# Attention and token-MLP on one core: scores one matmul ahead over five banks, and ScalarE's and the loads' order changed around the MLP

## The chip, the core and the metric

The kernel runs on one core of a Trainium2 chip. TensorE (PE) multiplies matrices into the eight banks of PSUM, ScalarE (ACT) computes functions and copies, VectorE (DVE) reduces and combines, GpSimd (POOL) works on on-chip memory alone, and SyncE (SP) issues transfers; ACT and POOL issue transfers too. Each engine runs its own queue of instructions in order and waits on semaphores for the others. The metric is the time of one execution on the device in microseconds (us); less is better.

## What is computed

```python
x = A_x                                       # 1 x 2048 x 640
g = sigmoid((x * gate_w).sum(-1, keepdims=True))
# a: attention with 32 heads of 20 channels
q, k, v = split(x @ wqkv)                     # 32 heads each
p = softmax(einsum("bhqd,bhkd->bhqk", q, k) * 20 ** -0.5)
a = concat_heads(p @ v) @ wo
# b: an MLP over the tokens, shared by the channels
h = layernorm(x)
u = gelu(einsum("bsd,sf->bdf", h, w1) + b1)   # F = 1728
b = (einsum("bdf,fs->bds", u, w2) + b2) transposed to tokens x channels
out = g * a + (1 - g) * b
```

Inputs and output are float32. Products that need more than one pass of the fast format are made of a high and a low part: `a = ah + al`, and `ah*bh + ah*bl + al*bh`.

## The kernel before, in words

The program has four stages that follow one another on TensorE.

**Projections (0 to 226 us).** Ten blocks of 128 rows of Q and K transposed, four tiles of 512 tokens each (`qk_unit`, L286: 15 matmuls), and V in two halves. The first two blocks of Q and of K come first, then V, then the rest. Each tile of Q and K is split into a high part (ACT, tile `evh`) and a low part (DVE, `evl`) and stored to DRAM by SP; for the first three K blocks (384 rows, `c` = 0 to 2) SP also stores them to `kd_d`, and for every second tile the difference to the tile before it (`kf`, `dh`). There are two buffers of `evh` and `evl` each and one of `kf`, so the next use of a buffer waits for its stores. V needs its own weights split (`split_wv`, L357) by ACT and DVE, in the same queues. Mean and variance of the layer norm, and the gate `g_t`, are made beside V (L378 to 414).

**MLP (226 to 774 us)**, in two halves `d` of 320 channels (`mlp`, L577). In each half `u` has 14 tiles of 128 hidden units and `y` 16 tiles of 128 tokens. Each step is one `pair64`: two matmuls of 64 rows that run side by side. The weights come in 120 chunks a half: `w_raw` (L450) loads chunk k into a `wr` tile, `w_split` (L462) makes its high part on ACT (`wh`) and its low part on POOL (`wl`), `w_need` keeps loads nine and splits four chunks ahead. Chunks 0 to 3 (`AHEAD = 4`) are fetched by ACT's queue during the projections into tiles that exist by then; from chunk 4 on, `wr`, `wh` and `wl` lie in the pool `gp`, which takes over the memory of the projections' pool `p1` (L510 to 513). `u_evac` (L526) copies a finished pair of sums on ACT, and puts off the rest through the list `soon`: POOL's addition after 6 steps, the Gelu (`u_gelu`, L545) after 18. `settle` (L518) counts `soon` down once a step. At the end of each `y` tile, `y_evac` does the same; in the first half the input of the second is loaded, normalised on DVE and split beside it (`h_load`, `h_norm`, `h_split`), with the last two splits behind the loop (L621 to 624).

Beside the MLP runs the first part of a second stream, the row maxima of the attention scores: `s_next` (L166) issues one matmul `s` of 512 columns (L193) and what reads it. They come two at a time, 1082 over the 2592 steps. For half of the heads three in eight go through ACT (`s_over`: a Relu into the tile `ov`, L206) and then DVE (`s_two`); the others are reduced by DVE alone (L199). Four PSUM banks rotate for `s`. A Relu stands in ACT's queue where its matmul was issued.

**Attention loop (774 to 1779 us).** 16 pairs of heads, 32 iterations `it` each. An iteration takes 128 keys and 1024 queries: four score matmuls `st` (L789; heads j = 0, 1, whose rows 0 and 64 let a neighbour run beside them), an exponential of each on ACT into a tile `p` (L792), two matmuls of the maxima of a later pair in between as long as there are any (`s_next`; the turn of j keeps neighbours on different rows), and then `pv_flush` (L720): the products with V of the iteration before, four tiles `p` by two passes each. Banks: `st` rotates over four (`tag="st", bufs=4`), but the third score of each iteration has a bank of its own (`s3`); two are for `s` and one for `pv`.

**Output projection (1779 to 1863 us)**, with the gate and the MLP's result added by DVE.

What sets the order: PE's instructions stand as written throughout, ACT's and DVE's from L325, POOL's and SP's from L417 on. So a wait at the head of one queue holds all that is written behind it.

## Time and profile before

| | us |
|---|---|
| three runs | 1860.23, 1867.78, 1869.33 (median 1867.78) |
| the profiled execution | 1864.34 |
| its span, first to last instruction | 1862.6 |
| busy in it: PE | 1832.7 (98%) |
| ACT | 1510.6 (81%) |
| DVE | 1241.1 (67%) |
| POOL | 632.2 (34%) |
| PE's weight loads, beside its matmuls | 1121.4 (60%) |

How to read the rows: L12 is line 12 of the kernel. A group's row has engine, operation, output<-inputs, shapes and count; a timeline's row has start and duration in us, then the same, and in brackets how long the engine was idle before and what ended that; a row of waits has who waited for whom, the total in us, how often, and the longest. PEld are PE's weight loads, SPq and ACTq what those queues issue. Matmuls overlap, so PE counts as busy where it is not at its full rate.

### The profile page before, as it was taken

The page shows a single profiled execution, that of the slowest core. Times are in us where ns is not written, and L with a number is a line of the kernel's source. Part 1 is how long each engine was busy: PE and PEld are TensorE (multiplying, and loading weights), DVE is VectorE, ACT ScalarE, POOL GpSimd, SP SyncE. Part 2 cuts the span into 40 slices and gives each one's busy share as a digit, 9 for nine tenths or more (in the row PEclk, how much of TensorE's full clock was granted, in tenths as well). Part 3 has the DMA queues.
Part 4 walks back from the last instruction along what each step waited for, and adds up shares of the span by engine and source line. Part 5 has one row for each costly group of instructions (what it writes and reads, how often), then busy time and mean ns, then how long its engine had stood idle before and what let it go on. Part 6 is the DMA issues. An engine that isn't in the chain of part 4 may idle for free. (4 is left out here: it accounts for less than half of the span.)

```text
span 1862.6 us, 40444 instructions
## 1 busy us (share of the span) xinstructions
PE 1832.7 (98%) x14978; PEld 1121.4 (60%) x14978; DVE 1241.1 (67%) x2407; ACT 1510.6 (81%) x3046; POOL 632.2 (34%) x882
## 2 busy tenths in 40 slices
PE   9999999999999999999999999999999999999998
PEld 7898789999899999633333333333333333333278
DVE  5303278898888888866666666666766666667137
ACT  4244378887788777599999999999999999999920
POOL 1012367778777767302111211121322121212210
PEclk9999999999999999999999999999999999999999
DMA  9657866466665555225222232142263322201363
GB/s 310 196 163 235 257 155 174 134 166 194 183 168 148 148 148 168 72 58 137 58 46 61 60 80 57 27 109 59 52 126 67 71 62 57 71 14 23 129 215 132
DMA packets 156695, 223.00 MB, mean 120 GB/s; under 512 B 65998, under 2 KB 92382, under 8 KB 153070
## 3 DMA queue, kind: packets, MB, share of 16 engines
q1 hardware_dynamic: 133888, 186.94, 36.8%
q0 software_dynamic: 13824, 18.81, 4.5%
q10 hardware_dynamic: 8784, 14.65, 2.4%
q8 instruction: 118, 1.93, 0.4%
q14 instruction: 81, 0.66, 0.1%
HBM read 165.43 MB, written 54.54 MB: 118 GB/s over the span
## 5 line engine op out<-in xcount | busy, mean ns | idle before, releaser
L199 DVE TENSOR_REDUCE mx<-s 128x1 f32<-128x512 f32 x1280 | 832.8, 686 | 303.8 <-PE st L789 165.1
L792 ACT ACTIVATE p<-st 128x512 f32<-128x512 f32 x2048 | 1004.0, 822 | 0.0
L726 PE MATMUL pv<-p,v 128*32 128x512 f32 x4096 | 567.6, 605 | 0.1
L789 PEld LDWEIGHTS st<-qs_True,ks_True 62*128 62x128 f32 x2048 | 245.9, 184 | 530.2 <-issue 426.8
L789 PE MATMUL st<-qs_True,ks_True 62*128 62x512 f32 x2048 | 508.9, 436 | 0.1
L193 PE MATMUL s<-ks_False,qs_False 60*128 60x512 f32 x1152 | 326.1, 407 | 15.0 <-ACT ov L206 10.6
L193 PE MATMUL s<-sk,sq 60*128 60x512 f32 x896 | 325.0, 442 | 0.0
L43 POOL TENSOR_TENSOR wl<-wr,wh 128x512 fp32r<-128x512 f32 x228 | 276.6, 1217 | 119.0 <-ACT wh L40 75.5
L213 DVE CUSTOM_DVE_ANT_0 ov<-s,ov 128x512 f32<-128x512 f32 x384 | 263.5, 687 | 60.2 <-PE s L193 54.0
L206 ACT ACTIVATE ov<-s 128x512 f32<-128x512 f32 x384 | 224.9, 597 | 84.0 <-PE s L193 79.6
L713 POOL DMA_DIRECT2D o_d<-oev x128 | 66.8, 522 | 619.7 <-DVE oev L707 603.8
L48 PE MATMUL y<-gh,wh 64*128 64x320 f32 x896 | 203.5, 307 | 0.0
L48 PE MATMUL y<-gl,wh 64*128 64x320 f32 x832 | 195.2, 307 | 0.0
L48 PE MATMUL y<-gh,wl 64*128 64x320 f32 x832 | 194.2, 306 | 0.0
L193 PEld LDWEIGHTS s<-ks_False,qs_False 60*128 60x128 f32 x1152 | 171.2, 185 | 30.4 <-ACT ov L206 17.5
L40 ACT ACTIVATE wh<-wr 128x512 fp32r<-128x512 f32 (+2 forms) x246 | 147.2, 601 | 46.4 <-DMA wr<-in_wqk_dram 31.0
L726 PEld LDWEIGHTS pv<-p,v 128*32 128x32 f32 x4096 | 102.2, 108 | 125.9 <-issue 116.7
L48 PE MATMUL u<-hl,wh 64*128 64x320 f32 x864 | 166.3, 307 | 0.0
L48 PE MATMUL u<-hh,wh 64*128 64x320 f32 x864 | 166.3, 307 | 0.0
L48 PE MATMUL u<-hh,wl 64*128 64x320 f32 x800 | 155.4, 307 | 0.0
L48 PEld LDWEIGHTS y<-gh,wh 64*128 64x128 f32 x896 | 143.6, 185 | 0.9
L48 PEld LDWEIGHTS y<-gl,wh 64*128 64x128 f32 x832 | 134.8, 185 | 0.7
(124 smaller groups left out, 2123.0 us busy)
## 6 DMA issues: line engine op xcount, KB each, us to landing
wr<-in_w_dram SPq DMA_DIRECT2D x196, 256.0 KB
ks_True<-k_d SPq DMA_DIRECT2D x96, 160.0 KB
qs_True<-q_d SPq DMA_DIRECT2D x192, 80.0 KB
qs_False<-q_d SPq DMA_DIRECT2D x108, 80.0 KB
sk<-k_d SPq DMA_DIRECT2D x42, 160.0 KB
sq<-q_d SPq DMA_DIRECT2D x84, 80.0 KB
v_d<-vt SPq DMA_DIRECT2D x32, 168.0 KB
v<-v_d SPq DMA_DIRECT2D x16, 336.0 KB
```

Of the source, the lines that this page charges most:

```text
L40: nc.scalar.activation(hi, src, AF.Copy)
L43: (lo_eng or nc.vector).tensor_sub(lo, src, hi.bitcast(F32))
L48: nc.tensor.matmul(ps[k], a[r], b[r], start=start, stop=stop)
L193: nc.tensor.matmul(ps, qs[half][r, t * P:(t + 1) * P], ks[r, kc * 512:(kc + 1) * 512], start=True, stop=True)
L199: nc.vector.tensor_reduce(mx[:, slot, j, t: t + 1], ps, axis=AX.X, op=OP.max)
L206: nc.scalar.activation(over[j, kc], ps, AF.Relu)
L213: nc.vector.tensor_tensor_reduce(ov, ps, ov, 1.0, -3.0e38, OP.add, OP.max, mx[:, slot, j, t: t + 1])
L713: nc.gpsimd.dma_start(o_d[DH * h: DH * h + DH, cols], ev[r: r + DH, :])
L726: nc.tensor.matmul(pv[r: r + 32, :], v_tiles[p][:, kt, 10 * j: 10 * j + 32], pts[j, c], start=(kt == 0), stop=(kt == NT - 1))
L789: nc.tensor.matmul(ps, ks[r, kt * P:(kt + 1) * P], qs[qh][r, c * 512:(c + 1) * 512], start=True, stop=True)
L792: nc.scalar.activation(pt, ps, AF.Exp, scale=SCALE)
```

## The change

Seven edits. (1) A score matmul `st` and its exponential are issued one place earlier: the first of iteration n stands before the `pv` of iteration n-2 instead of after it. The order of the heads within an iteration becomes 1, 0, 1, 0, and the scores rotate over five banks one after the other (`st0` to `st3` and `s3`); the tag `st` is cut into four tags of one bank, whose order of use elsewhere is as before. (2) A Relu of the maxima is issued two steps after its matmul. (3) Gelu comes 30 steps behind its tile instead of 18, but for the last of a half. (4) The second half's inputs are loaded three tiles ahead, normalised one ahead and split in the step of their own tile. (5) Weight chunks 4 to 7 are fetched by ACT's queue, into six tiles (`q4`) that held weights of the projections, and chunk 3 is split before the last Q/K tile. (6) The Gelu table is loaded right after the gate, by a Gelu of a tile that nobody reads any more (`ssq`), and the Exp table at the second half's fifteenth output tile instead of its fourth. (7) For the first two K blocks the four stores of the differences go through POOL's queue.

```diff
     def st_tile(shape, name):
-        return psum.tile(shape, F32, tag="st", bufs=4, name=name)
+        n = st_count[0] % 4
+        st_count[0] += 1
+        return psum.tile(shape, F32, tag=f"st{n}", bufs=1, name=name)
...
     def s_over(p, half, t, j, kc, over):
         def f():
             ps = s_mm(p, half, t, j, kc)
-            over[j, kc] = s_pool[0].tile([P, 512], F32, tag="over", bufs=3, name=f"ov{p}_{half}_{t}_{j}_{kc}")
-            nc.scalar.activation(over[j, kc], ps, AF.Relu)
+
+            def relu():
+                over[j, kc] = s_pool[0].tile([P, 512], F32, tag="over", bufs=3, name=f"ov{p}_{half}_{t}_{j}_{kc}")
+                nc.scalar.activation(over[j, kc], ps, AF.Relu)
+
+            soon.append([2, relu])
         return f
...
-        nc.sync.dma_start(kd_d[0, rows, cols], hi.bitcast(F32))
-        nc.sync.dma_start(kd_d[1, rows, cols], lo.bitcast(F32))
+        put = nc.gpsimd.dma_start if c < 2 else nc.sync.dma_start
+        put(kd_d[0, rows, cols], hi.bitcast(F32))
+        put(kd_d[1, rows, cols], lo.bitcast(F32))
...
-        nc.sync.dma_start(kd_d[0, rows, cols], dh.bitcast(F32))
-        nc.sync.dma_start(kd_d[1, rows, cols], kd)
+        put(kd_d[0, rows, cols], dh.bitcast(F32))
+        put(kd_d[1, rows, cols], kd)
...
     nc.vector.tensor_mul(b2o, b2_t, omg)
+    nc.scalar.activation(ssq, ssq, AF.Gelu_apprx_tanh)
...
         if k < AHEAD:
             raw = p1.tile([P, 4, P], F32, tag="xr", bufs=2, name=f"wr{k}")
+        elif k < 2 * AHEAD:
+            raw = q4([P, 4, P], F32, f"wr{k}")
         else:
             raw = gp.tile([P, 4, P], F32, tag="wr", bufs=8, name=f"wr{k}")
-        (nc.scalar if k < AHEAD else nc.sync).dma_start(raw[:, :n, :m], src)
+        (nc.scalar if k < 2 * AHEAD else nc.sync).dma_start(raw[:, :n, :m], src)
...
+        if n == 23:
+            w_split(3)
         qk_unit(m, w[m], q)
...
-        if n in (22, 23):
-            w_split(n - 20)
+        if n == 22:
+            w_split(2)
+            w_raw(4)
+            w_raw(5)
...
-            soon.append([18, lambda: u_gelu(f, xg, gh, gl)])
+            soon.append([18 if f == f_order[-1] else 30, lambda: u_gelu(f, xg, gh, gl)])
...
             for f in f_order:
+                if d == 0 and f == f_order[-1]:
+                    for i in range(3):
+                        h_load(1, i)
...
-                if d and t == 3:
+                if d and t == NT - 2:
                     nc.scalar.activation(eps_t, eps_t, AF.Exp)
                 if d == 0:
-                    if t > 1:
-                        hs[t - 2] = h_split(1, t - 2)
-                    if t > 0:
-                        h_norm(1, t - 1)
-                    h_load(1, t)
-            if d == 0:
-                hs[NT - 2] = h_split(1, NT - 2)
-                h_norm(1, NT - 1)
-                hs[NT - 1] = h_split(1, NT - 1)
+                    if t == 0:
+                        h_norm(1, 0)
+                    if t + 1 < NT:
+                        h_norm(1, t + 1)
+                    hs[t] = h_split(1, t)
+                    if t + 3 < NT:
+                        h_load(1, t + 3)
...
+    def st_op(i):
+        g, n = divmod(i, 4)
+        p, it = divmod(g, 32)
+        qh, kt = divmod(it, NT)
+        ks, qs = st_src[p]
+        j, c = 1 - n % 2, n // 2
+        r = slice(64 * j, 64 * j + 3 * DH + 2)
+        ps = psum.tile([P, 512], F32, tag="s3" if i % 5 == 4 else f"st{i % 5}", bufs=1, name=f"st{p}_{it}_{j}{c}")
+        nc.tensor.matmul(ps, ks[r, kt * P:(kt + 1) * P], qs[qh][r, c * 512:(c + 1) * 512], start=True, stop=True)
+        pt = lp.tile([P, 512], F32, tag="pt", bufs=12, name=f"p{p}_{it}_{j}{c}")
+        nc.scalar.activation(pt, ps, AF.Exp, scale=SCALE)
+        pts.setdefault(g, {})[j, c] = pt
+
+    st_op(0)
...
             for n in range(4):
-                st_op((n + turn) % 2, n // 2, s3_tile if n == 2 else st_tile)
+                i = 4 * (p * 32 + it) + n + 1
+                if i < NP * 128:
+                    st_op(i)
                 if n < take:
                     s_next()
...
-            pend.append((p, qh, kt, pv, pts))
+            pend.append((p, qh, kt, pv, pts.pop(p * 32 + it)))
```

Three places show how instructions move. First ACT where the projections end and the MLP begins; `evh9_3` is the high part of the last Q/K tile, `ov` a Relu, `wr4` to `wr7` are weight chunks 4 to 7 and `wh4` the split of chunk 4. Before:

```order
L40 ACTIVATE wtmp1_1440<-wr2_2097 128x512 [waits DMAHW5_49]
L40 ACTIVATE evh9_3_2163<-qk9_3_2147 128x512 [waits DMAHW3_49,DVE_49,PE_49]
L40 ACTIVATE wtmp1_1440<-wr3_2121 128x512 [waits DMAHW2_49]
L206 ACTIVATE ov0_0_0_1_0_2192<-s0_0_0_1_0_2190 128x512 [waits PE_49]
L206 ACTIVATE ov0_0_0_1_2_2204<-s0_0_0_1_2_2202 128x512 [waits PE_49]
L206 ACTIVATE ov0_0_0_0_0_2224<-s0_0_0_0_0_2222 128x512 [waits PE_49]
L40 ACTIVATE wh4_2232<-wr4_2177 128x512 [waits DMAHW4_49,DMAHW5_49,DMAHW1_49,DMAHW6_49,DMAHW0_49,DMAHW7_49,DVE_49,Pool_49]
L206 ACTIVATE ov0_0_1_1_0_2260<-s0_0_1_1_0_2258 128x512 [waits PE_49]
```

And with the change:

```order
L40 ACTIVATE wtmp1_1441<-wr2_2098 128x512 [waits DMAHW5_49]
L471 DMA wr4_2148<-in_w1_dram 128x512
L471 DMA wr5_2150<-in_w1_dram 128x512
L40 ACTIVATE wtmp1_1441<-wr3_2122 128x512 [waits DMAHW2_49]
L40 ACTIVATE evh9_3_2170<-qk9_3_2154 128x512 [waits DMAHW3_49,DVE_49,PE_49]
L471 DMA wr6_2182<-in_w1_dram 128x512 [waits DMAHW1_49]
L471 DMA wr7_2184<-in_w1_dram 128x512
L212 ACTIVATE ov0_0_0_1_0_2197<-s0_0_0_1_0_2191 128x512 [waits PE_49]
L212 ACTIVATE ov0_0_0_1_2_2212<-s0_0_0_1_2_2203 128x512 [waits PE_49]
L212 ACTIVATE ov0_0_0_0_0_2229<-s0_0_0_0_0_2223 128x512 [waits PE_49]
L40 ACTIVATE wh4_2233<-wr4_2148 128x512 [waits DMAHW5_49,DMAHW4_49,DMAHW6_49,DMAHW2_49,DMAHW7_49,DVE_49,Pool_49]
L212 ACTIVATE ov0_0_1_1_0_2268<-s0_0_1_1_0_2259 128x512 [waits PE_49]
```

Four loads came into ACT's queue, two of them between the last Q/K tile and the first Relu; the split of chunk 4 keeps its place and a list of waits, since its output lies in memory that the projections use.

Second, ACT in the first half's `u`, at the Gelu of tile 4 (`xg0_4`). Before:

```order
L40 ACTIVATE wh28_3409<-wr28_3151 128x512
L206 ACTIVATE ov0_1_7_1_0_3423<-s0_1_7_1_0_3421 128x512
L546 ACTIVATE xg0_4_3345<-xg0_4_3345,b1_t_83 128x320
L40 ACTIVATE gh0_4_3343<-xg0_4_3345 128x320
L206 ACTIVATE ov0_1_7_1_2_3443<-s0_1_7_1_2_3441 128x512
L40 ACTIVATE wh29_3456<-wr29_3202 128x512
```

And with the change:

```order
L40 ACTIVATE wh28_3410<-wr28_3152 128x512
L212 ACTIVATE ov0_1_7_1_0_3431<-s0_1_7_1_0_3422 128x512
L212 ACTIVATE ov0_1_7_1_2_3448<-s0_1_7_1_2_3439 128x512
L40 ACTIVATE wh29_3454<-wr29_3201 128x512
L212 ACTIVATE ov0_1_7_0_0_3471<-s0_1_7_0_0_3465 128x512
L562 ACTIVATE xg0_4_3346<-xg0_4_3346,b1_t_83 128x320
```

The Gelu and the copy `gh` went behind two more Relus and a split.

Third, PE in one iteration of the loop; the digits of a score are pair, iteration, head and half of the queries. Before:

```order
L193 MATMUL s12_1_3_1_3_21393<-sk12_18505,sq12_1_18507 128x512 [waits DVE_49]
L789 MATMUL st8_19_10_21396<-qs8_True_1_20084,ks8_True_20082 128x512 [waits Activation_49]
L193 MATMUL s12_1_3_0_3_21400<-sk12_18505,sq12_1_18507 128x512 [waits DVE_49]
L789 MATMUL st8_19_01_21403<-qs8_True_1_20084,ks8_True_20082 128x512 [waits Activation_49]
L789 MATMUL st8_19_11_21407<-qs8_True_1_20084,ks8_True_20082 128x512
L726 MATMUL pv8_1_21299<-p8_18_00_21364,v8_20268 32x512
L726 MATMUL pv8_1_21299<-p8_18_01_21378,v8_20268 32x512
L726 MATMUL pv8_1_21299<-p8_18_10_21371,v8_20268 32x512
L726 MATMUL pv8_1_21299<-p8_18_11_21382,v8_20268 32x512 [waits Activation_49]
L789 MATMUL st8_20_00_21415<-qs8_True_1_20084,ks8_True_20082 128x512
```

And with the change:

```order
L787 MATMUL st8_19_00_21394<-qs8_True_1_20089,ks8_True_20087 128x512 [waits Activation_49]
L197 MATMUL s12_1_3_1_3_21398<-sk12_18510,sq12_1_18512 128x512 [waits DVE_49]
L787 MATMUL st8_19_11_21401<-qs8_True_1_20089,ks8_True_20087 128x512 [waits Activation_49]
L197 MATMUL s12_1_3_0_3_21405<-sk12_18510,sq12_1_18512 128x512 [waits DVE_49]
L787 MATMUL st8_19_01_21408<-qs8_True_1_20089,ks8_True_20087 128x512 [waits Activation_49]
L787 MATMUL st8_20_10_21412<-qs8_True_1_20089,ks8_True_20087 128x512 [waits Activation_49]
L743 MATMUL pv8_1_21304<-p8_18_00_21369,v8_20273 32x512
L743 MATMUL pv8_1_21304<-p8_18_01_21383,v8_20273 32x512
L743 MATMUL pv8_1_21304<-p8_18_10_21361,v8_20273 32x512
L743 MATMUL pv8_1_21304<-p8_18_11_21376,v8_20273 32x512
```

The first score of iteration 20 moved ahead of the `pv` of iteration 18; each score now waits for the exponential that read its bank, and `pv` waits for none of its own.

More of the change, by code (lines that the diff above doesn't have):

```diff
@@ L71, in st_tile @@
     def st_tile(shape, name):
-        return psum.tile(shape, F32, tag="st", bufs=4, name=name)
+        n = st_count[0] % 4
+        st_count[0] += 1
+        return psum.tile(shape, F32, tag=f"st{n}", bufs=1, name=name)
+    st_count = [0]
     def s_tile(shape, name):
@@ L721, in pv_flush @@
         while pend:
-            p, qh, kt, pv, pts = pend.pop(0)
+            p, qh, kt, pv, pt = pend.pop(0)
             for j in range(2):
@@ L725, in pv_flush @@
                     r = 32 * (2 * j + c)
-                    nc.tensor.matmul(pv[r: r + 32, :], v_tiles[p][:, kt, 10 * j: 10 * j + 32], pts[j, c],
+                    nc.tensor.matmul(pv[r: r + 32, :], v_tiles[p][:, kt, 10 * j: 10 * j + 32], pt[j, c],
                                      start=(kt == 0), stop=(kt == NT - 1))
@@ L757, in o_late @@
         return o_part(q, slice((NC - 1) * P, D), 1, 512, "l", 4, nc.scalar, nc.vector)[0]
-    turn = given = 0
+    given = 0
+    pts = {}
+    def st_op(i):
[11 more added lines that the diff above has]
+    st_op(0)
     LEFT = NP * 128 + 2 - S_AHEAD
     for p in range(NP):
-        ks, qs = st_src[p]
+        qs = st_src[p][1]
         if 8 <= p < 8 + NC:
@@ L783, in gated_mix @@
                 pv = psum.tile([P, 512], F32, tag="pv", bufs=1, name=f"pv{p}_{qh}")
-            pts = {}
-            def st_op(j, c, tile):
-                r = slice(64 * j, 64 * j + 3 * DH + 2)
-                ps = tile([P, 512], f"st{p}_{it}_{j}{c}")
-                nc.tensor.matmul(ps, ks[r, kt * P:(kt + 1) * P], qs[qh][r, c * 512:(c + 1) * 512],
-                                 start=True, stop=True)
-                pt = lp.tile([P, 512], F32, tag="pt", bufs=12, name=f"p{p}_{it}_{j}{c}")
-                nc.scalar.activation(pt, ps, AF.Exp, scale=SCALE)
-                pts[j, c] = pt
             take = min(LEFT - given, 2)
             for n in range(4):
-                st_op((n + turn) % 2, n // 2, s3_tile if n == 2 else st_tile)
+                i = 4 * (p * 32 + it) + n + 1
+                if i < NP * 128:
+                    st_op(i)
                 if n < take:
@@ L802, in gated_mix @@
                 s_finish()
-            turn = (turn + take) % 2
             pv_flush()
```

## The prediction

> **What bounds the kernel now.** I read the windows of 100 us first, then the groups and one iteration of the attention loop on the timeline, then the waits of TensorE window by window. Columns of a window: its length, busy us (instructions) of PE, weight loads, DVE, ACT and POOL, granted clock, DMA share, GB/s.
>
> ```profile
> core 0: 1862.6 us, clock 0.995
> 300.00:400.00 100.00, 99.49 (x1215) 97.25 (x1214) 87.66 (x223) 81.23 (x162) 75.85 (x80) 1.00 0.57 156
> 900.00:1000.00 100.00, 100.00 (x719) 34.99 (x717) 68.74 (x113) 100.00 (x205) 18.37 (x40) 1.00 0.33 75
> L792 ACT ACTIVATE p<-st x2048: 592/827/858, 774.4 to 1777.5; 128x512 f32<-128x512 f32 x187
> ```
>
> There are two regimes. Up to 774 us TensorE has matmuls without pause and the others serve it; from 774.4 to 1777.5 us ScalarE computes 2048 exponentials, and is busy 100 of 100 us. The first stage can gain where TensorE waits; the loop only if an exponential's turn gets shorter.
>
> Whether it can is read from runs of exponentials that nothing separates: the first with score and maximum matmuls beside it, the second after those have run out. A run of n lasts n-1 turns and one full length (0.83).
>
> ```profile
> 1299.62 7.20 ACT L792 ACTIVATE p<-st 128x512 f32<-128x512 f32 x14
> 1737.39 23.36 ACT L792 ACTIVATE p<-st 128x512 f32<-128x512 f32 x47
> 575.08 1.07 ACT L206 ACTIVATE ov<-s 128x512 f32<-128x512 f32 x2
> ```
>
> (7.20-0.83)/13 = 0.490 us, and (23.36-0.83)/46 = 0.490 us, though TensorE's work differs. Two Relus of this size in the MLP, back to back: 1.07 less one of 0.59 is 0.48. So 0.49 is ScalarE's own pace; 2048 x 0.490 = 1003.5 us is the whole loop (1777.5-774.4 = 1003.1 from first start to last).
>
> The Trainium skill ("ScalarE: Activation LUTs", What happens when an `exp` ACTIVATE runs) states one element per cycle and lane once the pipe is full, 0.833 ns. By that the estimate is 512 x 0.833 = 427 ns a turn; the trace shows 490, and nothing of this size under 0.48.
>
> **The loop.** An iteration in TensorE's rows:
>
> ```profile
> 1301.48 0.19 PEld L789 LDWEIGHTS st<-qs_True,ks_True 62*128 62x128 f32 x2 [0.19 <-ACT p L792]
> 1301.91 0.20 PEld L726 LDWEIGHTS pv<-p,v 128*32 128x32 f32 x8 [0.24 <-issue]
> 1302.95 0.18 PEld L789 LDWEIGHTS st<-qs_True,ks_True 62*128 62x128 f32 x1 [0.84 <-issue]
> 1303.29 0.40 PE L789 MATMUL st<-qs_True,ks_True 62*128 62x512 f32 x1
> 1303.44 0.19 PEld L789 LDWEIGHTS st<-qs_True,ks_True 62*128 62x128 f32 x2 [0.19 <-ACT p L792]
> 1303.52 0.42 PE L789 MATMUL st<-qs_True,ks_True 62*128 62x512 f32 x2
> ```
>
> From one 1301.48 to the next 1303.44 is 1.96 us = 4 x 0.49: last pair of scores to pv 0.43, pv 1.04, first pair 0.34, second to third pair 0.15. TensorE waits 0.19 of it for an exponential, so its own chain lies between 1.77 and 1.96. With the change the four scores, two maxima and pv remain, shifted by one score; the fifth-last exponential now frees the last score's bank, and the same exponential frees pv. A score has one turn (0.49) more in hand, and ScalarE loses the extra semaphore instructions that stand before half of its exponentials, but the turn was 0.490 with them. I take 0.4 us of gain, for starts that come late once in a while; bounds: 0, and 2048 x (0.490-0.48) = 20 us if the Relus' pace were reachable.
>
> **Start of the MLP: the fifth weight chunk.** ACT and SP, then the waits and the windows:
>
> ```profile
> 233.06 3.65 SPq L459 DMA_DIRECT2D wr<-in_w_dram  x8
> 229.03 0.62 ACT L40 ACTIVATE wtmp<-wr 128x512 fp32r<-128x512 f32 x1
> 229.55 1.77 ACT L206 ACTIVATE ov<-s 128x512 f32<-128x512 f32 x3
> 236.35 0.63 ACT L40 ACTIVATE wh<-wr 128x512 fp32r<-128x512 f32 x1 [5.03 <-DMA wr<-in_w_dram]
> PEld s L193 <- ACT ov L206: 5.2, 2, 3.6
> 226.00:254.00 28.00, 22.57 (x230) 20.65 (x230) 16.03 (x38) 16.59 (x31) 12.73 (x11) 0.88 0.55 170
> 254.00:282.00 28.00, 27.95 (x336) 27.08 (x335) 24.00 (x62) 21.68 (x46) 20.15 (x24) 1.00 0.74 170
> 236.00:243.00 7.00, 5.48 (x38) 5.20 (x40) 2.70 (x7) 3.74 (x7) 3.80 (x3) 0.51 0.89 272
> ```
>
> Weight loads from chunk 4 on go out at 233.06, when the memory of the stage before is free; the split of chunk 4 waits until 236.35, a Relu is queued behind it, and TensorE stands 3.6 us for that Relu (of 5.2 in two waits from 228 to 244; the other, 1.6, is for the first Relu). Then it runs at a granted 0.51. 230 matmuls in 28 us, where the next 28 us do 336: 28 - 230/12 = 8.8 us lost. Chunks 4 to 7 now land in the older buffers, but their split still writes into the freed memory, so it can start at about 233.1 instead of 236.35: 3.3 us of the 3.6. The half clock fills 236 to 243, with TensorE busy for 5.48 of it: 2.7 us, which goes too if the wait shrinks to tenths. What is late next: the four loads (1 MB) now run beside the last stores, whose landing frees the memory; at 272 GB/s they take 3.9 us, of which I charge 0.8. And two of their issues (0.33 each on ScalarE) stand before the first Relu, where TensorE waits 1.6 already: 0.3 more, as one chunk's split, 0.62, moves ahead of it. SP has four issues fewer (3.65/8 = 0.46 each), so chunk 8 lands sooner. Together 3.3+2.7-0.8-0.3 = 4.9; bounds: 0 (the release as late as the load was) and 8.8.
>
> The Trainium skill ("TensorE: Matmul & The Clock Gate", Part 1) says that an idle window of about 3.4 us halves the clock until one such window was busy. The wait of 3.6 with 0.51 behind it agrees. If a wait that long stayed, the 2.7 would stay with it, and the sum would be 2.7 smaller.
>
> **Activation tables.** Both loads now stand where ScalarE idles: Gelu's after the gate, with 2.90 us of idle time soon behind it, Exp's after the second half's fifteenth output tile, ahead of 8.37 us.
>
> ```profile
> 247.77 1.28 ACT L546 ACT_TABLE_LOAD   x1
> 671.34 1.28 ACT L614 ACT_TABLE_LOAD   x1
> PEld s L193 <- ACT ov L206: 1.2, 1, 1.2
> PEld s L193 <- ACT ov L206: 1.6, 1, 1.6
> 153.11 0.60 ACT L40 ACTIVATE evh<-qk 128x512 fp32r<-128x512 f32 x1 [2.90 <-PE qk L54]
> 773.47 0.62 ACT L565 ACTIVATE ty<-y,b2o,omg 128x320 f32<-128x320 f32 x1 [8.37 <-PE y L48]
> ```
>
> TensorE's two waits are those of 249 to 252 and of 672 to 675. If the cover were gone, each load would cost its 1.28. Gain 1.1+1.5 = 2.6 (a weight load's wait is some 0.1 longer than TensorE's); between 1 and 2.8.
>
> **Gelu 30 steps behind its tile instead of 18.**
>
> ```profile
> 295.95 0.56 ACT L546 ACTIVATE xg<-xg,b_t 128x320 f32<-128x320 f32 x1 [1.74 <-POOL xg L530]
> ACT xg L546 <- POOL xg L530: 9.1, 12, 1.9
> PEld s L193 <- ACT ov L206: 1.7, 1, 1.7
> ```
>
> ScalarE waits 12 times for GpSimd's addition, and the Relu behind it holds TensorE: 1.7 here (294 to 299), and in the same way 1.2, 0.4, 0.4, 0.4 and 0.5 in five other places of the second half. Twelve steps more are 2.0 us (336 matmuls, two a step, in 28 us), longer than GpSimd's longest delay, 1.9. Gain 4.6 less 0.2 each: 3.5; from 1.5 to 4.6.
>
> **Second half's inputs loaded and normalised earlier.**
>
> ```profile
> 505.76 0.45 DVE L430 TENSOR_SCALAR xm<-xm,negm,rstd 128x320 f32<-128x320 f32 x1 [2.49 <-DMA xm<-in_x_dram]
> PEld s L193 <- DVE mx L213: 2.8, 1, 2.8
> ```
>
> The last normalisation waits for its load and TensorE for VectorE. With loads three tiles ahead this is gone: 2.7, from 2 to 2.8. On SP such a load may now wait for its buffer, with weight loads behind it; those run eight chunks ahead.
>
> **Relus two steps later.** Between two steps ScalarE may get a group of output work ahead of a Relu that used to follow it. TensorE's waits for Relus are 17.5 us in 25 cases between 226 and 740; those above are 3.6+1.2+1.6+4.6 and the first 1.6, so 4.9 stay. Against that stand idle times of ScalarE before Relus:
>
> ```profile
> PEld s L193 <- ACT ov L206: 17.5, 25, 3.6
> ACT ov L206 <- PE s L193: 79.6, 160, 2.4
> ```
>
> I put the edit at 0, between 4.9 gained and 4.9 lost; it is hidden as long as the four banks of s leave a Relu some 1.6 us (1082 maxima over 2592 steps put four into 9.6 steps).
>
> **Stores of the K differences on GpSimd's queue.** Sixteen of SP's stores move.
>
> ```profile
> 62.22 1.05 SPq L313 DMA_DIRECT2D kd_d<-kf  x1
> 67.25 0.69 DVE L303 COPY kf<-qk 128x512 f32<-128x512 f32 x1 [1.50 <-DMA kd_d<-kf]
> PEld v L54 <- DVE wv L43: 2.7, 2, 2.2
> 64.00:76.00 12.00, 8.20 (x36) 7.17 (x35) 4.23 (x8) 2.99 (x6) 0.00 (x0) 0.72 0.95 277
> 76.00:88.00 12.00, 12.00 (x82) 12.00 (x82) 2.36 (x9) 3.70 (x9) 0.79 (x6) 1.00 0.21 75
> xn<-in_x_dram POOLq DMA_DIRECT2D x4, 320.0 KB, 6.1
> ```
>
> Before V, TensorE waits for V's weights, VectorE's part of them behind a copy that waits for such a store (issued 62.22, free 67.25). 12 - 36/6.83 = 6.7 us is the loss (82 matmuls in 12 us are 6.83 a us), half clock included. GpSimd can issue as soon as its data stand, about 0.3 to 1.8 us earlier, but the DMA engines are 95% busy and a GpSimd load took 6.1 us there against 5.0 for this store. I take 1.5; from -1.3 to 6.4. The skill's main page ("Trainium Kernel Development and Optimization", Key Constraints) says that issuing from several queues saves only the sequencer's time; by that the term would be 0.
>
> **Sum.** 0.4+4.9+2.6+3.5+2.7+0+1.5 = 15.6 us. The profiled execution took 1864.34 us with a span of 1862.6: 1848.7. The runs' median, 1867.78, is 3.4 above it, giving 1852.2; between the two I say 1850. The raw maxima from 740 to 774, paced by VectorE, and the output projection are untouched.
>
> **Rivals.** (1) *Moved, not removed*: the freed memory comes as late as the load did (0 of 4.9) and the Relus give back 4.9; what stays is 15.6-4.9-4.9 = 5.8, or 1860. For it: the split's wait on all those stores is in both orders. Against: the loads took the 3.3 us by their own rows.
> (2) *Slower: the loop becomes TensorE's.* The last score waits for its bank while its partner has gone ahead, so the two no longer run side by side: another 0.23 (1303.52 after 1303.29), against the 0.19 that TensorE waits today. With 0.07 us an iteration over 1.96: 512 x 0.07 = 36, less 15.6: 1886. It decides from 1.99 us an iteration on (15.6/512 = 0.03). Against: by the rows the partner arrives within 0.05 of the bank.
> (3) *The turn shrinks*: 0.48 would add 20: 1830; the skill's bare 427 ns would give 2048 x 0.063 = 129 less, which the two runs of 0.490 speak against.
> (4) *Nothing*: the waits removed were covered by DMA time: 1866. The granted clock of 0.51 speaks against.
>
> **Chances.** Forecast 0.60 (own range 1843 to 1859), (1) 0.18, (2) 0.12, (3) 0.06, (4) 0.04. About 0.5% (9.3 us) is what a measurement tells from no change: faster 0.65, the same 0.22, slower 0.13. The range 1839 to 1866 leaves out most of (2) and (3).
>
> **What would show it.** Right: exponentials still 0.490 apart; no table load between 226 and 740; wh of chunk 4 before 234.5 and PEclk 1.00 from 230 to 250; the loop's first exponential near 759. Wrong: iterations other than 1.96, TensorE's waits for Relus above 10 us in the MLP, or 64 to 76 us slower than now.

## The result, and the profile after

Twelve runs of the changed kernel have a median of 1864.18 us (1860.42 to 1870.41), twelve of the kernel before 1866.40 (1860.23 to 1869.33). The ratio is 0.9989, interval 0.9977 to 1.0002: a gain of 2 us that can't be told from none, where 15.6 were forecast. The profiled execution took 1860.53 us with a span of 1858.7, at the fast end of its runs; a second one 1866.67.

The rows that answer to those of before. Windows of the changed kernel, columns as in the prediction:

```profile
226.00:254.00 28.00, 26.54 (x266) 24.48 (x266) 18.48 (x44) 17.55 (x35) 13.17 (x11) 0.94 0.66 204
236.00:243.00 7.00, 7.00 (x71) 6.53 (x69) 4.71 (x12) 4.26 (x8) 3.80 (x3) 0.83 0.61 194
64.00:76.00 12.00, 8.34 (x38) 6.80 (x37) 5.17 (x9) 3.64 (x8) 3.25 (x6) 0.94 0.84 272
300.00:400.00 100.00, 98.45 (x1198) 96.55 (x1196) 88.01 (x221) 80.80 (x161) 76.10 (x79) 1.00 0.58 162
```

The start of the MLP does more in its 28 us (266 matmuls for 230). But the MLP begins 2.8 us later (below), and from 300 to 400 us TensorE is busy for less than before (98.45 for 99.49). The waits of 226 to 740 us:

```profile
PEld s L197 <- ACT ov L212: 15.4, 27, 1.5
```

TensorE's waits for Relus are 15.4 us in 27 cases where they were 17.5 in 25: the long ones have gone, and short ones came. The prediction had named more than 10 us of them as a sign that it was wrong. The page's group of the exponentials, and then their runs on the timeline with the Exp table's load:

```profile
L789 ACT ACTIVATE p<-st 128x512 f32<-128x512 f32 x2048 | 1003.6, 940 | 0.6 <-PE st L787 0.6
```

```profile
1732.36 28.37 ACT L789 ACTIVATE p<-st 128x512 f32<-128x512 f32 x57
760.54 1.28 ACT L633 ACT_TABLE_LOAD   x1
```

ScalarE waited 0.6 us for scores in all of the loop. (28.37-0.94)/56 = 0.490 us a turn, unchanged. The table load stands where ScalarE had been idle, and there is none between 226 and 740 us, as forecast.

To see where time is won or lost, four marks are read from the timeline of each execution: the MLP's first matmul `u`; the start of the first copy of a finished pair of sums (`xg`); the way from there to the start of the last output copy (`ty`); and the way from the loop's first exponential to its last.

| profile (us) | first `u` | first `xg` | `xg` to last `ty` | loop |
|---|---|---|---|---|
| before | 226.5 | 244.7 | 528.7 | 1003.1 |
| before, once more | 226.1 | 243.1 | 531.3 | 1004.6 |
| changed | 229.3 | 243.1 | 526.2 | 1002.7 |
| changed, once more | 230.2 | 246.7 | 527.0 | 1003.8 |
| relu_now | 230.0 | 247.7 | 517.7 | 1005.3 |
| kd_on_sp | 228.7 | 245.9 | 525.7 | 1002.7 |
| relu_now_kd_sp | 226.1 | 245.4 | 517.9 | 1002.7 |
| gelu18 | 228.8 | 244.6 | 533.8 | 1002.7 |
| gelu18_relu_now_kd_sp | 226.3 | 244.7 | 525.4 | 1002.7 |
| first_weights_old | 227.8 | 246.1 | 519.1 | 1002.7 |
| fifth_split_own_memory | 227.1 | 245.3 | 517.4 | 1002.7 |
| loop_old | 229.4 | 249.7 | 518.2 | 1002.7 |
| relu_late_first | 228.1 | 246.9 | 519.2 | 1003.8 |
| relu_late_first_weights_old | 227.6 | 246.2 | 519.6 | 1003.8 |
| gelu_table_on_demand | 230.1 | 247.0 | 523.8 | 1002.7 |
| gelu_table_in_wait | 227.8 | 243.7 | 519.7 | 1003.5 |
| gelu_table_in_wait_weights_old | 228.1 | 245.0 | 519.5 | 1003.5 |
| before_gelu_table_at_gate | 227.0 | 247.0 | 528.7 | 1002.8 |

The names are those of the experiments below. Means of the two executions each: up to the first `xg` the change has lost 1.0 (243.9 to 244.9), where 6.4 were forecast to be gained; from there to the last `ty` it has gained 3.4 (530.0 to 526.6), where 8.8 were.

### The profile page after: what moved, and what is told of

It is laid out like the page before. It is cut to its first block, busy times and chain, and to the rows that moved or that the text cites. A ratio compares the mean times of both kernels' runs of the same rounds, so it can differ in the third digit from the quotient of the medians.

```text
span 1858.7 us, 39442 instructions
## 1 busy us (share of the span) xinstructions
PE 1829.8 (98%) x14978; PEld 1188.1 (64%) x14978; DVE 1239.4 (67%) x2407; ACT 1511.7 (81%) x3047; POOL 640.8 (34%) x898
## 5 line engine op out<-in xcount | busy, mean ns | idle before, releaser
L787 PEld LDWEIGHTS st<-qs_True,ks_True 62*128 62x128 f32 x2048 | 336.0, 185 | 462.6 <-ACT p L789 434.7
L743 PE MATMUL pv<-p,v 128*32 128x512 f32 x4096 | 546.6, 605 | 0.2 <-PE st L787 0.2
L787 PE MATMUL st<-qs_True,ks_True 62*128 62x512 f32 x2048 | 529.3, 437 | 1.1 <-ACT x L556 1.1
L197 PE MATMUL s<-ks_False,qs_False 60*128 60x512 f32 x1152 | 315.2, 407 | 9.7 <-ACT ov L212 8.4
L48 PE MATMUL y<-gh,wh 64*128 64x320 f32 x896 | 196.7, 307 | 0.0
L48 PE MATMUL y<-gl,wh 64*128 64x320 f32 x832 | 188.3, 307 | 0.0
L48 PE MATMUL y<-gh,wl 64*128 64x320 f32 x832 | 186.5, 306 | 0.0
L197 PEld LDWEIGHTS s<-ks_False,qs_False 60*128 60x128 f32 x1152 | 164.6, 185 | 24.0 <-ACT ov L212 15.4
L743 PEld LDWEIGHTS pv<-p,v 128*32 128x32 f32 x4096 | 81.2, 108 | 125.1 <-issue 115.6
L197 PEld LDWEIGHTS s<-sk,sq 60*128 60x128 f32 x896 | 130.7, 184 | 0.0
```

The source lines that it names most:

```text
L48: nc.tensor.matmul(ps[k], a[r], b[r], start=start, stop=stop)
L197: nc.tensor.matmul(ps, qs[half][r, t * P:(t + 1) * P], ks[r, kc * 512:(kc + 1) * 512], start=True, stop=True)
L743: nc.tensor.matmul(pv[r: r + 32, :], v_tiles[p][:, kt, 10 * j: 10 * j + 32], pt[j, c], start=(kt == 0), stop=(kt == NT - 1))
L787: nc.tensor.matmul(ps, ks[r, kt * P:(kt + 1) * P], qs[qh][r, c * 512:(c + 1) * 512], start=True, stop=True)
```

## The experiments

**The Relus and the stores.** *relu_now*: the changed kernel, with

```diff
-            soon.append([2, relu])
+            relu()
```

> The changed kernel with its Relus issued right behind their matmul again, as before. Theory (the later Relus gave back what the MLP gained): TensorE's waits for Relus between the first half's first and last output tile, 8.5 us in the changed kernel and 3.9 before, fall to 4 or less; the stretch from the first to the last of these tiles, 128.2 us in the changed kernel and 125.5 before, falls to 125 or less; the whole is 3 to 5 us shorter than the changed kernel, 1860. Rival (the inputs' splits, which now stand in the same step as the output copies, hold the Relus): the stretch stays at 128, the whole at 1864.

Measured: 1858.59 us (6 runs), ratio to the kernel before 0.9956 (0.9939 to 0.9972). The first half's output tiles, first to last copy, take 125.5 us. Waits of TensorE's weight loads for Relus between 365 and 510 us, first of the kernel before:

```profile
PEld s L193 <- ACT ov L206: 3.9, 11, 0.7
```

Of the changed kernel:

```profile
PEld s L197 <- ACT ov L212: 8.5, 14, 1.5
```

And with the Relus at once:

```profile
PEld s L197 <- ACT ov L212: 3.6, 11, 0.7
```

The theory holds: the waits are 3.6 (4 or less was expected), the tiles are as long as before the change (125 or less was expected), and the whole is 5.6 us shorter, more than the 3 to 5 of the theory. What stands in ScalarE's queue at the end of an output tile shows why. The changed kernel first:

```profile
398.82 0.62 ACT L581 ACTIVATE ty<-y,b2o,omg 128x320 f32<-128x320 f32 x1 [0.33 <-PE y L48]
399.34 0.52 ACT L556 ACTIVATE x<-y,omg 128x320 f32<-128x320 f32 x1
399.75 0.47 ACT L40 ACTIVATE hh<-xm 128x320 fp32r<-128x320 f32 x1
400.11 0.41 ACT L40 ACTIVATE wh<-wr 128x256 fp32r<-128x256 f32 x1
400.42 1.08 ACT L212 ACTIVATE ov<-s 128x512 f32<-128x512 f32 x2
401.06 0.18 PEld L197 LDWEIGHTS s<-ks_False,qs_False 60*128 60x128 f32 x1 [1.00 <-ACT ov L212]
```

And the same place with the Relus at once:

```profile
401.33 0.60 ACT L212 ACTIVATE ov<-s 128x512 f32<-128x512 f32 x1
401.83 0.61 ACT L581 ACTIVATE ty<-y,b2o,omg 128x320 f32<-128x320 f32 x1
402.33 0.53 ACT L556 ACTIVATE x<-y,omg 128x320 f32<-128x320 f32 x1
402.74 0.48 ACT L40 ACTIVATE hh<-xm 128x320 fp32r<-128x320 f32 x1
403.10 0.42 ACT L40 ACTIVATE wh<-wr 128x256 fp32r<-128x256 f32 x1
403.41 0.60 ACT L212 ACTIVATE ov<-s 128x512 f32<-128x512 f32 x1
404.13 0.18 PEld L197 LDWEIGHTS s<-ks_False,qs_False 60*128 60x128 f32 x1 [0.42 <-DVE mx L203]
```

A Relu whose matmul was issued just before a tile's end now falls behind the tile's two copies and two splits, and meets the next Relu there: two stand in a row behind 1.6 us of other work, and TensorE waits 1.00 us. At once, one goes ahead of that group.

The output tiles are not the only place. Between the two executions that differ in the Relus alone and have their stores on SyncE (kd_on_sp and relu_now_kd_sp, below), undoing the edit takes 0.6 us out of the first half's `u`, 2.7 out of its output tiles, 3.5 out of the second half's `u` and 1.3 out of its output tiles; the stretch between the halves is 0.3 longer. In the second half's `u` the same thing happens at the end of a tile of hidden units: in the changed kernel two Relus stand in a row at 605.77, behind two copies and a split that begin at 604.60, and TensorE waits 0.70; with the Relus at once, one of them starts at 603.28, ahead of the copies.

*kd_on_sp* and *relu_now_kd_sp*: the stores of the K differences on SyncE's queue again, alone and with the Relus at once.

```diff
-        put = nc.gpsimd.dma_start if c < 2 else nc.sync.dma_start
+        put = nc.sync.dma_start
```

> The changed kernel with all stores of the K differences on SyncE's queue again. Theory (GpSimd's stores compete with the loads of the projections' weights): the wait of 3.0 us for a weight split at 49 to 52 us is gone, the first product of V starts at 64.8 us as before instead of 68.4, the MLP at 226.5 instead of 229.3; the whole is 2.8 us shorter than the changed kernel, 1861. Rival (the late weight load was chance of that one execution): the first product of V starts anywhere between 64.8 and 68.4 and the median stays at 1864.

> Both undone. If both theories hold the two gains add, since one lies in the projections and one in the MLP: 1864.2 - 4 - 2.8 = 1857.4, ratio to the kernel before 0.995. If both rivals hold: 1864, ratio 0.999.

Measured: 1864.32 us (12 runs), ratio 0.9989 (0.9980 to 0.9999), and 1855.53 (6 runs), 0.9946 (0.9928 to 0.9965). Alone the edit is worth nothing in the median, as its rival has it; beside the Relus at once 3 us, with intervals that overlap those of relu_now. Read the other way, the Relus at once are worth 8.8 us here, where they were worth 5.6 with GpSimd's stores; in the MLP of the profiles (first `xg` to last `ty`, in the table) it is 7.8 and 8.5. In kd_on_sp the first product of V starts at 65.1 us, as expected (68.4 in the changed kernel), but the MLP at 228.7 and not at 226.5. In the table, the first `u` stands at 229.6 on the mean of the four profiles with GpSimd's stores (228.8 to 230.2) and at 227.6 on that of the fourteen with SyncE's (226.1 to 230.1): the stores on GpSimd seem to delay the projections by some 2 us, but the two ranges overlap. By the first `xg` the difference has gone (means 245.5 and 245.8).

**The Gelu.** *gelu18*: the changed kernel with Gelu 18 steps behind its tile; *gelu18_relu_now_kd_sp*: the same on relu_now_kd_sp, which is the base of the rest.

```diff
-            soon.append([18 if f == f_order[-1] else 30, lambda: u_gelu(f, xg, gh, gl)])
+            soon.append([18, lambda: u_gelu(f, xg, gh, gl)])
```

> The changed kernel with Gelu 18 steps behind its tile again. Theory (the later Gelu is worth what it was priced at): TensorE's waits of 1.7 near 297 us and 1.2 near 567 us come back, and the whole is 2.5 to 3.5 us longer, 1867. Rival (waits removed from the MLP are made up for by its next stretch, which runs faster after a stall): the waits come back but the last output tile ends within 0.5 us of the changed kernel's, and the whole stays at 1864.

> Relus at once, the K stores on SyncE, and Gelu 18 steps behind its tile again. Theory (the later Gelu's worth is its own waits, 2.1 near 297 us, 1.3 near 338, 1.7 near 571): 4 to 6 us longer than 1855.5, 1860.5. Rival (the 8.9 us between the changed kernel and its variant with Gelu at 18 came from both edits together, Relus two steps late meeting the early Gelus): with Relus at once only the prediction's 3.5 us or less is left, 1859 or below.

Measured: 1873.04 us (7 runs), ratio 1.0033 (1.0020 to 1.0047), and 1863.35 (11 runs), 0.9988 (0.9979 to 0.9997). The later Gelu is worth 8.9 us with the late Relus and 7.8 without: its own price, not one of both together, and twice the 3.5 of the prediction. It is also more than either expectation had, and the rivals fall. In the table 525.4-517.9 = 7.5. Waits for Relus with Gelu at 18, from 245 to 365 and from 510 to 740 us:

```profile
PEld s L197 <- ACT ov L212: 2.9, 5, 1.7
PEld s L197 <- ACT ov L212: 4.9, 7, 1.8
```

The same two with Gelu at 30:

```profile
PEld s L197 <- ACT ov L212: 0.9, 1, 0.9
PEld s L197 <- ACT ov L212: 0.2, 1, 0.2
```

2.0+4.7 = 6.7 us of waits. The prediction had counted 4.6; the wait of 1.8 near 510 us is missing there, since in the kernel before TensorE stands at that place for the late input (2.8).

**The first weight chunks.** *first_weights_old*: chunks 4 to 7 through SyncE as before.

```diff
-        elif k < 2 * AHEAD:
-            raw = q4([P, 4, P], F32, f"wr{k}")
-        (nc.scalar if k < 2 * AHEAD else nc.sync).dma_start(raw[:, :n, :m], src)
+        (nc.scalar if k < AHEAD else nc.sync).dma_start(raw[:, :n, :m], src)
...
-        if n == 23:
-            w_split(3)
...
-        if n == 22:
-            w_split(2)
-            w_raw(4)
-            w_raw(5)
+        if n in (22, 23):
+            w_split(n - 20)
```

> Relus at once and the K stores on SyncE (1855.5), and now the weight chunks 4 to 7 fetched as before too: by SyncE once the memory is free, chunk 3 split after the last Q/K tile. Theory (that edit moved the wait from the load to the last store, and the loads beside the stores made the store late): the split of chunk 4 comes 9.9 us after the MLP's first matmul as before, not 13.4; the stretch from that matmul to the first pair of sums copied is 18.2 as before against 19.4, and the whole is 0 to 3 us shorter than 1855.5. Rival (the edit is worth the 4.9 us that the prediction gave it): the whole is 1860.

Measured: 1858.24 us (5 runs), ratio 0.9963 (0.9950 to 0.9976), against the base's 0.9946 (0.9928 to 0.9965). That is 2.7 us longer than the base, where the theory had 0 to 3 shorter and the rival 4.9 longer. The intervals overlap; the 4.9 us (0.26%) are not excluded by them alone, but the profiles show none of it: the first `xg` comes 18.2 us after the first `u` as before (base 19.4), at 246.1 (base 245.4). The split of chunk 4 comes 12.3 us after the first `u` (base 13.4), not 9.9. ScalarE and SyncE in the base:

```profile
231.09 0.63 ACT L40 ACTIVATE wtmp<-wr 128x512 fp32r<-128x512 f32 x1 [1.30 <-DMA wr<-in_w_dram]
232.44 0.60 ACT L40 ACTIVATE evh<-qk 128x512 fp32r<-128x512 f32 x1 [0.73 <-DMA k_d<-evh]
233.34 1.08 ACT L212 ACTIVATE ov<-s 128x512 f32<-128x512 f32 x2 [0.30 <-issue]
239.49 0.63 ACT L40 ACTIVATE wh<-wr 128x512 fp32r<-128x512 f32 x1 [4.08 <-DMA k_d<-evl]
233.79 0.32 SPq L306 DMA_DIRECT2D k_d<-evl  x1
233.99 0.28 PEld L197 LDWEIGHTS s<-ks_False,qs_False 60*128 60x128 f32 x1 [4.84 <-ACT ov L212]
```

The split of chunk 4 now waits for the last store instead of its load, until 239.49; before, that moment was 236.35, load included. The store goes out at 233.79, 5.7 us before the split starts. And the first Relus stand behind two instructions that wait for transfers themselves, so TensorE stands 4.84 us for the first Relu, where it stood 1.6.

*fifth_split_own_memory*: chunks 4 and 5 early, and the parts of chunk 4 in two of the older buffers.

```diff
-        elif k < 2 * AHEAD:
+        elif k < AHEAD + 2:
...
+        elif k == AHEAD:
+            hi, lo = q4([P, 4, P], F32R, f"wh{k}"), q4([P, 4, P], F32R, f"wl{k}")
```

> Relus at once, the K stores on SyncE; chunks 4 and 5 fetched by ScalarE's queue, and the high and low part of chunk 4 in two of the older buffers, so that its split waits for its load alone; chunk 5's split is the first to wait for the freed memory, chunks 6 and 7 come by SyncE. Theory (what holds ScalarE, and TensorE behind it, is the memory that the last store releases): the split of chunk 4 stands within 1 us behind the Relus ahead of it, the wait for the store is at chunk 5, TensorE's longest wait for a Relu falls from 4.9 to 3 or less, the whole to 1853. Rival (TensorE lacks the weights anyway, or ScalarE stands for something else): longest wait 4 us or more, 1855.

Measured: 1855.69 us (6 runs), ratio 0.9944 (0.9930 to 0.9957). The split of chunk 4 runs at 235.97, right behind the Relus, yet the time stays and TensorE's longest wait is 4.3 us:

```profile
234.65 0.29 PEld L197 LDWEIGHTS s<-ks_False,qs_False 60*128 60x128 f32 x1 [4.30 <-ACT ov L212]
```

This is the wait for the first Relu. The theory falls in what it says of TensorE: with the split's wait gone, the wait ahead of it decides.

**The loop.** *loop_old*: the base with the attention loop of before.

```diff
-                i = 4 * (p * 32 + it) + n + 1
-                if i < NP * 128:
-                    st_op(i)
+                st_op((n + turn) % 2, n // 2, s3_tile if n == 2 else st_tile)
```

> Relus at once, the K stores on SyncE, and the attention loop as before: four banks in rotation and one apart, scores behind the products with V. Theory (the loop is ScalarE's own pace of 0.490 us an exponential): exponentials 1003.1 us from the first start to the last start, 0.5 us more than with the change, and the first exponential 0.7 us sooner: the whole within 1 us of 1855.5. Rival (the five banks bring a shorter or longer turn): the loop differs by 5 us or more.

Measured: 1857.94 us (6 runs), ratio 0.9957 (0.9944 to 0.9970). The loop takes 1002.7 us with either order; the old one's first exponential comes 0.9 us after the last `ty`, the new one's 1.6. The five banks are worth nothing here. The median is 2.4 us above the base, more than the 1 us expected, but in the profile the difference stands ahead of the loop: the first `xg` comes at 249.7 (base 245.4).

**What the start has in common.** *relu_late_first*: the base with Relus two steps late for the first 20 maxima alone; *relu_late_first_weights_old*: the same with chunks 4 to 7 as before.

```diff
-            relu()
+            if s_count[0] <= 20:
+                soon.append([2, relu])
+            else:
+                relu()
```

> K stores on SyncE; Relus two steps late only for the first 20 maxima of the MLP (its first output tile), at once from there on. Theory (a late Relu helps where the last Q/K copy stands ahead of it, and costs everywhere else): the stretch from the MLP's first matmul to its first copied pair of sums, 18.2 to 20.3 us in the four executions with Relus at once and these stores, falls to 17.3 (as with all Relus late) or less; from there to the last output tile 518 us as with Relus at once, not 526; the whole 1.5 to 3 us shorter than 1855.5, 1853. Rival (the first tile's gain was chance of single executions): the stretch stays at 18.2 to 20.3, the whole at 1855.5.

> The same with weight chunks 4 to 7 fetched as before. Theory (the chunks fetched early bring nothing, since the split then waits for the last store): within 2 us of the run with the Relus late in the first tile alone. Rival (with the Relus late there the early chunks pay what the prediction gave them): 4.9 us longer.

Measured: 1858.43 us (5 runs), ratio 0.9961 (0.9949 to 0.9974), and 1858.24 (5 runs), 0.9953 (0.9939 to 0.9967). First `u` to first `xg`: 18.8 and 18.6 us. The theory of late Relus that help in the first tile falls: 17.3 or less was expected, and the median is 2.9 us above the base instead of 1.5 to 3 below. Without the early chunks the time is the same.

*before_again* and *after_again*, for their profiles:

> The kernel before once more, for its profile: how far the projections of one kernel differ between two executions. Theory (transfers make them vary by 1 to 3 us, the MLP and the loop repeat within 0.2): the MLP's first matmul between 225 and 229 (226.5 in the first profile), the stretches from the fourth pair of sums on and the loop within 0.2 of the first profile's. Rival: all stretches vary alike.

> The changed kernel once more, for its profile. Theory (stores on GpSimd's queue cost the projections 2 us): the MLP's first matmul between 228.5 and 230.5, as in the three executions with these stores on GpSimd (228.8, 229.3, 230.0), above the mean of those with SyncE (227.4). Rival (the difference is chance): at or below 227.4.

Measured: 1865.82 and 1866.67 us, one run each. The first `u` at 226.1 and 230.2, as expected of both. Most stretches of the MLP repeated within 0.2, but the theory of 0.2 for all of them falls: from the first half's last `ty` to the next `xg` the kernel before took 15.4 us instead of 12.8, and the changed one 10.7 instead of 10.0; the loop grew by 1.5 and 1.1 us (last section). In the kernel before TensorE's wait for the late input was the same in both executions, 2.8 and 2.9 us; but behind it the granted clock was 1.00 in the first, and 0.57 and 0.58 from 504 to 512 us in the second. The first `xg` differs by 1.7 and 3.6 us between two executions of one kernel.

*gelu_table_on_demand*: the base without the Gelu table's load at the gate; *gelu_table_in_wait*: the load where ScalarE waits for the last Q/K weights; *gelu_table_in_wait_weights_old*: that with chunks 4 to 7 as before; *before_gelu_table_at_gate*: the kernel before with the load at the gate and nothing else.

```diff
-    nc.scalar.activation(ssq, ssq, AF.Gelu_apprx_tanh)
...
-            w[units[n + 4][0]] = load_w(units[n + 4][0])
+            raw = w_dma(units[n + 4][0])
+            if n == 16:
+                nc.scalar.activation(eps_t, eps_t, AF.Gelu_apprx_tanh)
+            w[units[n + 4][0]] = load_w(units[n + 4][0], raw)
```

> Relus at once, K stores on SyncE, and no Gelu table load at the gate: it comes at the first Gelu as before. Theory (the table load at the gate puts off the first Q/K stores after it by about 1 us, in a stage whose end is set by the transfers): the first store behind the gate stands 7.0 us or less behind V's last matmul (7.9 with the load), the first copied pair of sums at 244 instead of 246; TensorE's wait of 1.2 near 249 us is back, so the whole is 1 us shorter to 0.5 longer than 1855.5. Rival (the table has nothing to do with it): first pair at 246, the whole 1 us longer.

> Relus at once, K stores on SyncE, the Gelu table loaded while ScalarE waits for the last Q/K weights (near 203 us, where it stands 5 to 7 us). Theory: first copied pair of sums at 244, no wait near 249, the whole 2 us shorter than 1855.5: 1853.5. Rival: first pair at 246, 1855.5.

> The same with weight chunks 4 to 7 fetched as before. Theory (the early chunks bring nothing, the last store sets the split): within 1.5 us of the run with the early chunks. Rival (they pay once the table is out of the way): 3 to 4.9 us longer.

> The kernel before with nothing but the Gelu table's load at the gate. Theory: first copied pair of sums at 246 instead of 244, then 0.7 to 1.2 us back where the wait near 249 us is gone; the whole 0.5 to 1.5 us longer than the kernel before. Rival (the load is hidden, as the prediction had it): first pair at 244, the whole 1.1 us shorter.

Measured, in this order: 1857.40 us (6 runs), ratio 0.9947 (0.9928 to 0.9966); 1855.12 (6), 0.9935 (0.9921 to 0.9950); 1855.94 (6), 0.9940 (0.9926 to 0.9954); 1865.11 (12), 0.9990 (0.9976 to 1.0004). The first `xg`: 247.0, 243.7, 245.0, 247.0. The second and fourth profile agree with the theory of the table, the first with its rival, and the fourth's median is 1.7 us below that of before, as the rival has it. So the table is not shown to be the cause. (Without the load the first store behind the gate did stand 6.2 us behind the start of V's last product, against 8.1 in the base, but the first `xg` came no sooner.) The early chunks are worth 2.7, -0.2 and 0.8 us by the medians of the three pairs of runs, 1.1 on the mean; the expected 4.9 came in none.

gelu_table_in_wait has the lowest median of all: 0.65% below the kernel before (0.50 to 0.79%). It is not told from its base, 0.4 us above it.

## Why the prediction was wrong, by its own steps

| term | forecast | measured | read from |
|---|---|---|---|
| loop | 0.4 | 0, and 0.7 lost at its start | loop_old |
| chunks 4 to 7, half clock | 4.9 | 1.1 (2.7, -0.2, 0.8) | three pairs of runs |
| Gelu and Exp tables | 2.6 | 2.4 | 0.9 and 1.5, tile by tile |
| Gelu 30 steps behind | 3.5 | 7.8 | gelu18_relu_now_kd_sp |
| inputs earlier | 2.7 | 2.8 with the Gelu's part, 1.3 without | last `ty` of the first half to the next `xg`: 12.8 before, 10.0 changed, 11.5 in gelu18_relu_now_kd_sp; one execution each |
| Relus two steps later | 0 | -5.6, and -8.8 with the stores on SyncE | relu_now; kd_on_sp against relu_now_kd_sp |
| stores on GpSimd | 1.5 | 0 (-3 beside the Relus at once) | kd_on_sp, relu_now |

The inputs were not undone in a run of their own, and the kernel before took 15.4 us for that stretch in its second execution, so their price is the least certain. With 1.3 for them, and with the Relus and the stores together at -8.7, the terms add up to 3.2 us; the two series of twelve runs differ by 2.2.

**The step that failed most** is "I put the edit at 0 [...]; it is hidden as long as the four banks of s leave a Relu some 1.6 us". The condition was the right one, and the rows to apply it were at hand: an output tile's end puts two copies and two splits into ScalarE's queue, 1.6 us by the rows above. A Relu that is moved two steps falls behind that group, and it takes a second one with it. (The 1.6 us are themselves too short: of the 336 matmuls in 28 us 59 are maxima, so 9.6 steps take about 1.9 us, and the edit uses two of these steps.) The loss went past the bound of 4.9, because that bound counted waits that stood in the profile and not those that a move can make: relu_now has 3.6+0.2 us of such waits from 365 us on, the changed kernel 8.5+4.6.

**The second** is "their split [...] can start at about 233.1 instead of 236.35: 3.3 us of the 3.6", with "of which I charge 0.8" for the loads beside the stores. The split did change from waiting for its load to waiting for the memory, but the memory came later by as much: at 237.83 in the changed kernel and 239.49 in the base. The transfers of 225 to 240 us, in the kernel before:

```profile
DMA packets 1891, 3.47 MB, mean 231 GB/s; under 512 B 204, under 2 KB 204, under 8 KB 1890
```

And in the changed one:

```profile
DMA packets 2125, 3.90 MB, mean 260 GB/s; under 512 B 232, under 2 KB 232, under 8 KB 2123
```

The loads that used to follow the last store now run beside it, in a stage that has moved 264 and 268 GB/s from 155 to 226 us. The three pairs of runs that differ in these chunks alone show what that costs. SyncE's first weight load goes out when the memory is free: 13.5, 12.9 and 10.0 us after the first `u` with the early chunks, 8.9, 9.3 and 6.3 without, so 3.6 to 4.6 us later. That uses up the load's time: the split of chunk 4 starts 1.2, 0.2 and 0.3 us later with the early chunks than without. The split in gelu_table_in_wait, where it waits for the store, and in gelu_table_in_wait_weights_old, where it waits for the load, with the first `u` at 227.8 and 228.1:

```profile
237.70 0.63 ACT L40 ACTIVATE wh<-wr 128x512 fp32r<-128x512 f32 x1 [4.47 <-DMA k_d<-evl]
237.70 0.63 ACT L40 ACTIVATE wh<-wr 128x512 fp32r<-128x512 f32 x1 [5.51 <-DMA wr<-in_w_dram]
```

The charge should have been the loads' own 3.9 us and not the 0.8 that was taken: this is the first half of rival (1), "moved, not removed", for which the prediction named the rows and gave 0.18. Its second half, Relus that give back 4.9, came as well. That the order of the start matters little as a whole (first `xg` 243.1 to 249.7 us whatever was put where) was measured; which transfer makes it vary so between executions stays open. The best guess tried, the Gelu table, is neither shown nor excluded.

**A size that was off**: the Gelu. The mechanism was right, and the wait hidden behind the late input was not counted. (By the prediction's own rows, six places and 0.2 off each, the term was 3.4, and twelve steps are about 2.4 us rather than 2.0, for the same 59 maxima.)

**Right**: the turn of 0.490 us (rivals 2 and 3 did not come), both tables, and that the wait of 2.8 us for the late input goes; its price is not separated from the Gelu's.

**The half clock** did not go with the long wait. Windows of the changed kernel's profile:

```profile
232.00:234.00 2.00, 1.22 (x12) 0.96 (x12) 0.90 (x2) 1.69 (x3) 0.67 (x1) 1.00 1.02 381
236.00:238.00 2.00, 2.00 (x17) 2.00 (x15) 0.91 (x3) 0.17 (x1) 0.00 (x0) 0.50 0.39 151
```

Its waits there:

```profile
PEld s L197 <- ACT ov L212: 1.6, 2, 1.4
PEld s L197 <- DVE mx L203: 0.7, 1, 0.7
```

The clock is at 0.50 behind waits of 1.4 and 0.7 us, in which TensorE itself stood idle for 1.0 and 0.4 us. The prediction let the 2.7 us of the half clock go "if the wait shrinks to tenths", which it did not. Over the 18 us from the first `u` the mean granted clock is 0.81 in both executions of the kernel before, 0.91 in both of the changed one, and 1.00 in one profile alone, that of gelu_table_in_wait. The Trainium skill ("TensorE: Matmul & The Clock Gate", Part 1) asks for an idle window of about 3.4 us; this profile shows the half clock without one.

## What to carry to other kernels

An instruction that is moved a little later in an in-order queue has to be checked against the bursts of that queue, not against its idle time: what counts is the group it now falls behind, and whether it meets the next of its kind there. Where a stage is paced by transfers, as here, a load that is issued earlier can lengthen what runs beside it by as much as it saves; the wait moves to the other end. Edits of opposite sign that arrive together have to be taken apart one by one: here some 11 us of gain and 9 of loss looked like a change that does nothing.

## What was not expected of the hardware

TensorE's granted clock drops at the start of the attention loop in some executions and not in others of the same kernel, without a long idle time ahead: before the fall in relu_now no two matmuls start more than 1.4 us apart. The window at the loop's begin, of relu_now:

```profile
766.00:780.00 14.00, 13.55 (x69) 5.02 (x69) 7.31 (x14) 11.02 (x23) 1.31 (x3) 0.76 0.54 136
```

And of the changed kernel's first profile:

```profile
770.00:784.00 14.00, 13.53 (x91) 5.50 (x91) 9.45 (x17) 13.42 (x29) 1.55 (x4) 1.00 0.55 133
```

Where the clock fell (7 of 18 profiles, 0.79 to 0.89 over the first 16 us), ScalarE waits for scores there, and the loop takes 1003.5 to 1005.3 us; in ten of the other eleven it takes 1002.7 or 1002.8, with the old order and the new, and in one 1003.1. That is a spread of up to 2.6 us, and two executions of one kernel differ by 1.1 and 1.5; what decides it stays open.
